# Windowed attention and two MLPs on one core: two constants in the costs of a build-time planner

## The chip, the cores and the metric

One NeuronCore of a Trainium2 chip runs the program. Its engines work side by side: TensorE (PE in the profile, its weight loads PEld), VectorE (DVE), ScalarE (ACT), GpSimd (POOL), and SyncE (SP), which issues the transfers. The metric is the device time of one execution in microseconds (us), lower is better; several runs are made and their median is compared.

## What is computed

```python
def _attn_ref(q, k, v):                      # batch 4, heads 8, seq 576, head_dim 64
    scores = scale * np.matmul(q, k.transpose(0, 1, 3, 2))
    mask = (rel >= 0) & (rel < 64)           # each query sees 64 keys
    scores = np.where(mask, scores, -1000000000.0)
    attn = np.exp(scores - np.max(scores, axis=-1, keepdims=True))
    attn = attn / (np.sum(attn, axis=-1, keepdims=True) + 1e-09)
    return np.matmul(attn, v)

def _moe_ref(x, w_in, w_out, s, b):          # x: 2304 tokens x 512; w_in 512 x 2048; w_out 2048 x 512
    r = np.maximum(x @ w_in, 0.0)
    return (s * (r * r) + b) @ w_out

def _moe2_ref(x, w_in, w_out, alpha):        # the same sizes
    h = x @ w_in
    return (np.maximum(h, 0.0) + alpha * np.minimum(h, 0.0)) @ w_out

def reference(...):
    x = attention output as 2304 x 512
    return _moe2_ref(_moe_ref(x, ...), ...)
```

All tensors are float32.

## The kernel before, in words

Nearly float32 accuracy is kept on TensorE by splitting each operand into a high and a low part (hi and lo, in a rounded format) and by three matmuls for each product: hi·hi, hi·lo and lo·hi. So every activation and every weight needs, before TensorE can use it, a cast to its high part and a subtraction that leaves the low part. Those pairs are the bulk of the work of VectorE and ScalarE. Lines that make them are L641/L642 and L646 (attention's output), L694/L696 and L699 (sums of operands), L741 and its partner (output weights), and L1048 and L1051 (the hidden values). The cast may run on ScalarE or on VectorE, where the code offers both; the subtraction is always VectorE's.

The work goes through these stages. First comes attention in groups (scores L523, maximum L548, exponentials L562, the inverse of their sum L572 and L573, normalization L580 on GpSimd or VectorE, transposes L597 with copies L604/L605, values L628). The attention of the first token blocks takes up the first 60 us or so; that of the later ones runs in between the matmuls of the first MLP. The weights arrive packed as integers: they are loaded (L664, 128 x 4096 bytes each), and converted by L668 and L672 on ScalarE and L677, L678, L682 and L687 on VectorE. The first groups of the first MLP run as ordinary matmuls (hidden L1336, projection L1396). From about 230 us on, the hidden products are made pairwise in the manner of Strassen, seven products in the place of eight (`hidden_pair`, L978). There the partial product of one bank of PSUM is copied into the next bank by ScalarE (L989), and the next product is added onto it. The projection is L1419; its sums into the accumulators are L1462, L1496 and L1499. In the last groups the output is made by seven products as well (`output`, L1218, with copies L1232, sums L1242 and L1261).

What sets the order is a planner, `Plan`. The kernel first records steps. A step has one or more ways (engine, cost, code, tail), the steps that it depends on, and a due time `at`. `emit` then goes through all steps as a list scheduler does. For each step that is ready it works out the earliest start for each way, from the time when the engine is free and from the times when the inputs are done, plus a hop of 0.2 us where TensorE takes part and 0.1 to 0.12 us otherwise. It picks a way by a value that counts the cost several times (VectorE 1 + 3, ScalarE 1 + 2), takes the step that can start first, and among those of the engine the one with the earliest due time. The instructions are issued to each engine in the order found, and the engines then keep that order whatever the real times are. The lines that do the booking are:

```python
t = max((done[d] + hop(took[d], w[0]) for d in deps), default=0.0)
t = max(t, free.get(w[0], 0.0), after_)
value = t + w[1] * (1.0 + self.SPARE[w[0]]) + w[3]
free[eng] = t0 + cost
done[i0] = t0 + cost + tail
```

The cost and the tail of a step come from small helpers, `pe`, `act`, `dve`, `pool` and `dma`, from the number of columns. Some steps carry a tuple of their own: the maximum, the exponentials, the inverse, and the clamp and shift of the weights (L677, L678).

Of the kernel before, what the change touches and what calls it, by code (L numbers as in the profile page):

```python
# [47 lines left out]
LAG7, FORM = 2.15, 14.0  # L48
SOON7 = {(1, 2): (3.0, 0.0, 0.0), (1, 3): (0.0, 0.0, 12.0)}
SOON = 16.0  # L50
PAIR_AT = (0, 3584)
W_AT = (0, 1024, 2048, 3584, 4608, 5632)

# [195 lines left out]
def tile_window_attention_two_mlps(  # L249
# [69 lines left out]
        return [("pe", n * (0.0137 + cols * 0.000417), fn, 0.0)]  # L319

    def act(cols, fn):
        return ("act", 0.2 + cols * 0.00084, fn, 0.0)

    def dve(cols, fn, fast=False, port=False):
        return ("dve", 0.15 + cols * (0.00053 if fast else 0.00106), fn, 0.0) + (True,) * (fast or port)

    def pool(cols, fn):
        return ("pool", 0.1 + cols * 0.00184, fn, 0.0)
# [28 lines left out]
    with tc.manual_schedule():  # L357
# [94 lines left out]
        def group(gi, bi, hps, at1, at2):  # L452
# [44 lines left out]
            def before():  # L497
# [84 lines left out]
                for h in range(2):  # L582
                    T.step(
                        [dve(NP * P, lambda h=h: norm(nc.vector, h), port=True), pool(NP * P, lambda h=h: norm(nc.gpsimd, h))],
                        reads=[(den, 0), (den, 1)], writes=[(sm, h)], at=at1,
                    )

            def after():
# [13 lines left out]
                for h in range(2):  # L602
                    T.step(
                        [act(NP * P, lambda h=h: nc.scalar.copy(P_(h), Q_(h))),  # L604
                         dve(NP * P, lambda h=h: nc.vector.tensor_copy(P_(h), Q_(h)))],  # L605
                        reads=[pp[h]], writes=[pt[h]], at=at2,
                    )
# [29 lines left out]
                for t, hp in enumerate(hps):  # L637
                    xh, xl = f"xh{hp}.{bi}", f"xl{hp}.{bi}"
                    an = lambda t=t: A_(0)[:, t * n:(t + 1) * n].rearrange("p (c t) -> p c t", t=P)
                    T.step(  # L640
                        [act(n, lambda xh=xh, an=an: nc.scalar.copy(T[xh], an())),  # L641
                         dve(n, lambda xh=xh, an=an: nc.vector.tensor_copy(T[xh], an()))],  # L642
                        reads=[(av[0], t)], writes=[xh], at=at2,
                    )
                    T.step(
                        [dve(n, lambda xh=xh, xl=xl, an=an: nc.vector.tensor_sub(T[xl], an(), f32(T[xh])))],  # L646
                        reads=[(av[0], t), xh], writes=[xl], at=at2,
                    )
# [4 lines left out]
        def converted(layer, f, part, at, after):  # L653
# [12 lines left out]
            )  # L666
            T.step(
                [act(512, lambda: nc.scalar.activation(T[t], H().bitcast(F32), AF.Abs, scale=65536.0))],  # L668
                reads=[(raw, 1)], writes=[t], at=at, after=after,
            )  # L670
# [127 lines left out]
        def w_slot(n, k):  # L798
            lo, hi = PIECES[k]
            return T.place(f"W{k}.{n}", AW, PAIR_AT[n % 2] + 2 * lo * W2, 2 * (hi - lo) * W2, F32R)  # L800

# [98 lines left out]
        def x_pieces(q, at):  # L900


            t1, t2 = 2 * q * HALF, (2 * q + 1) * HALF
            AYv = AY.rearrange("p (k t) -> p k t", k=NK)
            B = lambda r, c: AYv[:, 2 * r:2 * r + 2, (t1, t2)[c]:(t1, t2)[c] + HALF]
            src = lambda r, c: [f"yh{k}.0.{2 * q + c}" for k in (2 * r, 2 * r + 1)]
            temps = {}

            def add(name, a, b, reads):
                t = T.place(f"T{name}.{q}", AS, name % 2 * C, C)  # L910
                temps[name] = t
                T.step(
                    [dve(C, lambda: nc.vector.tensor_sub(x2(T[t]), a(), b()), port=True)], reads=reads, writes=[t], at=at,
                )

            def piece(j, s, reads):
                x_stage(1, q, j, s, reads, at + ORDER.index(j) * PAIR / 7)

            tv = lambda n: (lambda: x2(T[temps[n]]))
            piece(1, lambda: B(0, 0), src(0, 0))  # L920
            add(1, lambda: B(0, 1), lambda: B(0, 0), src(0, 0) + src(0, 1))
            piece(5, tv(1), [temps[1]])
            add(2, lambda: B(1, 1), tv(1), src(1, 1) + [temps[1]])
            piece(6, tv(2), [temps[2]])
            piece(2, lambda: B(1, 0), src(1, 0))
            add(3, lambda: B(1, 1), lambda: B(0, 1), src(1, 1) + src(0, 1))
            piece(7, tv(3), [temps[3]])
            piece(3, lambda: B(1, 1), src(1, 1))
            add(4, lambda: B(1, 0), tv(2), src(1, 0) + [temps[2]])
            piece(4, tv(4), [temps[4]])  # L930
# [16 lines left out]
        def hidden_pair(layer, g, q, p):  # L947
# [8 lines left out]
            if p == 0 and x_load.held != (layer, q):  # L956
                x_load.held = (layer, q)
                if (layer, g) == (1, 0):
                    x_pieces(q, begin[1, 0, q] - SOON)
                for j in ORDER if (layer, g) != (1, 0) else ():  # L960
# [714 lines left out]
```

## Time and profile before

| what | us |
|---|---|
| runs of the kernel before | 840.16, 844.36, 844.75 |
| their median | 844.36 |
| the profiled execution | 840.98 |
| its span in the trace | 839.2 |

The span is the time between the first and the last recorded instruction of the profiled execution; the 1.8 us around it are not in the trace. In the views below an entry tells its start in us from the start of the span, its length in us, its engine, its line, the operation, the tile that it writes and the tiles that it reads, and how many instructions were put together (x3). In brackets stands the time that the engine stood idle right ahead of it, and behind an arrow the operation that ended the idle time.

### The profile page before, as it was taken

How to read it: one execution, taken by the hardware profiler on the slowest of the kernel's cores; microseconds unless marked ns; L12 is line 12 of the kernel's file. 1: busy time of each engine (PE TensorE's matmuls, PEld its weight loads, DVE VectorE, ACT ScalarE, POOL GpSimd, SP SyncE). 2: the span in 40 equal slices, each digit the busy share in tenths (PEclk: the TensorE clock that was granted, in tenths of full speed). 3: DMA queues.
4: the chain of work that ended last, by engine and by line, in shares of the span. 5: the costliest groups of instructions: out<-in, count | busy, mean ns of one | idle time of the engine just before them, and what ended most of it. 6: DMA issues, size and time to landing. Idle time of an engine off the chain costs nothing.

```text
span 839.2 us, 15002 instructions
## 1 busy us (share of the span) xinstructions
PE 824.7 (98%) x5517; PEld 775.7 (92%) x5521; DVE 693.1 (83%) x1210; ACT 536.9 (64%) x1219; POOL 106.1 (13%) x117
## 2 busy tenths in 40 slices
PE   8899999999999999999999999999999999999997
PEld 4678878888899999999999999999999999999997
DVE  6978799698987887699888999878888688778695
ACT  6878997554676555477648678778655345445461
POOL 6443344442011010011000000000000000000000
PEclk9999999999999999999999999999999999999999
DMA  8576974467558989958799668858998667438813
GB/s 287 183 229 176 297 222 131 184 235 284 212 204 314 376 312 316 411 186 339 282 382 380 227 248 309 320 183 303 345 389 314 230 225 268 123 121 338 319 42 109
DMA packets 72648, 217.25 MB, mean 259 GB/s; under 512 B 7424, under 2 KB 25984, under 8 KB 72576
## 3 DMA queue, kind: packets, MB, share of 16 engines
q1 hardware_dynamic: 72576, 216.31, 71.8%
q8 instruction: 43, 0.70, 0.3%
q14 instruction: 29, 0.24, 0.1%
HBM read 151.00 MB, written 65.27 MB: 258 GB/s over the span
## 4 chain that ended last, share of the span: by engine, by line
PE 76%; DVE 10%; DMA 6%; ACT 3%; POOL 3%; issue 1%; SPq 0%; DVEq 0%; POOLq 0%; ACTq 0%
PE y L1419 23%; PE h L978 17%; PE ab L978 13%; PE y L1218 11%; DMA raw<-w_in 3%; PE h L1336 3%; DMA xd<-aq 3%; PE y L1396 3%; PE y L628 2%; PE y L597 2%; PE ab L523 1%; DVE aq L699 1%; ACT as__86 L562 1%; POOL as__86 L580 1%; DVE ag L1051 1%
## 5 line engine op out<-in xcount | busy, mean ns | idle before, releaser
L1419 PE MATMUL y<-ax,woh 128*128 128x384 f32 x864 | 196.2, 334 | 0.0
L978 PE MATMUL h<-ax,aw 128*128 128x384 f32 x936 | 184.4, 334 | 0.7 <-ACT h L989 0.6
L978 PEld LDWEIGHTS h<-ax,aw 128*128 128x128 f32 x936 | 164.2, 188 | 1.6 <-ACT h L989 0.9
L1419 PEld LDWEIGHTS y<-ax,woh 128*128 128x128 f32 x864 | 153.7, 188 | 0.5 <-DVE ay L1496 0.3
L978 PE MATMUL ab<-ax,aw 128*128 128x384 f32 x702 | 139.7, 335 | 1.1 <-ACT h L989 0.9
L978 PEld LDWEIGHTS ab<-ax,aw 128*128 128x128 f32 x702 | 123.1, 188 | 2.4 <-ACT h L989 1.6
L1419 PE MATMUL y<-ax,wol 128*128 128x384 f32 x432 | 121.2, 334 | 0.0
L1336 PE MATMUL h<-ax,aw 128*128 128x512 f32 (+1 forms) x360 | 83.9, 377 | 1.1 <-DVE ax L646 1.1
L1419 PEld LDWEIGHTS y<-ax,wol 128*128 128x128 f32 x432 | 79.0, 188 | 0.0
L1336 PEld LDWEIGHTS h<-ax,aw 128*128 128x128 f32 x360 | 62.0, 189 | 12.8 <-DVE ax L646 1.5
L1051 DVE TENSOR_TENSOR ax<-r,ax 128x384 fp32r<-128x384 f32 x108 | 57.9, 553 | 5.7 <-ACT ax L1048 5.2
L668 ACT ACTIVATE raw<-raw 128x512 f32<-128x512 f32 x64 | 43.2, 679 | 28.8 <-DMA raw<-w_in 16.5
L1006 DVE TENSOR_TENSOR aq<-ab,aq 128x768 f32<-128x768 f32 x39 | 37.3, 955 | 15.7 <-PE ab L978 11.9
L1062 ACT ACTIVATE r<-r 128x384 f32<-128x384 f32 (+2 forms) x90 | 47.5, 543 | 1.1
L580 POOL TENSOR_TENSOR as__86<-as__86,den 128x512 f32<-128x512 f32 x36 | 40.3, 1142 | 56.2 <-DVE den L573 34.1
L682 DVE SCALAR_TENSOR_TENSOR raw<-raw 128x512 int32<-128x512 int32 x64 | 46.3, 725 | 1.2 <-ACT raw L672 1.2
L1058 ACT ACTIVATE r<-h 128x384 f32<-128x384 f32 (+2 forms) x57 | 29.7, 521 | 27.4 <-PE h L1336 17.6
L1499 DVE TENSOR_TENSOR ay<-y,ay 128x384 f32<-128x384 f32 x72 | 37.7, 553 | 9.6 <-PE y L1419 9.5
L733 POOL TENSOR_TENSOR wsum<-wsum,raw 128x512 f32<-128x512 f32 x15 | 21.9, 1459 | 181.6 <-DVE raw L687 180.1
L687 DVE CUSTOM_DVE_ANT_0 raw<-raw 128x1024 uint16<-128x1024 uint16 x64 | 44.7, 704 | 0.1
L672 ACT ACTIVATE raw<-raw 128x512 int32<-128x512 uint32 x64 | 43.0, 680 | 2.4 <-DMA raw<-w_in 1.6
L1218 PE MATMUL y<-ax,woh 128*128 128x384 f32 (+1 forms) x183 | 41.3, 333 | 0.6 <-ACT y L1232 0.6
(164 smaller groups left out, 1493.7 us busy)
## 6 DMA issues: line engine op xcount, KB each, us to landing
ax<-xd SPq DMA_DIRECT2D x91, 768.0 KB, 6.3
aw<-wd SPq DMA_DIRECT2D x33, 512.0 KB, 5.1
raw<-w_in SPq DMA_DIRECT2D x32, 512.0 KB, 6.9
raw<-w_out SPq DMA_DIRECT2D x32, 512.0 KB, 5.5
xd<-ax SPq DMA_DIRECT2D x21, 768.0 KB, 4.5
wd<-ag SPq DMA_DIRECT2D x30, 512.0 KB, 6.6
xd<-aq SPq DMA_DIRECT2D x12, 768.0 KB, 4.1
xd<-ax SPq DMA_DIRECT2D x36, 192.0 KB, 4.6
```

Of the source, the lines that this page charges most:

```text
L580: eng.tensor_mul(x, x, d)
L668: [act(512, lambda: nc.scalar.activation(T[t], H().bitcast(F32), AF.Abs, scale=65536.0))],
L672: [act(512, lambda: nc.scalar.activation(L(), L().bitcast(U32), AF.Copy, scale=2.0 ** -29))],
L682: [dve(512, lambda: nc.vector.scalar_tensor_tensor(out=L(), in0=H(), scalar=-0x80000000, in1=L(), op0=ALU.bitwise_and, op1=ALU.bitwise_or) ...
L687: [dve(512, lambda: nc.vector.tensor_tensor(ti(), ti(), L(), op=ALU.add), port=True)],
L978: nc.tensor.matmul(bank(), W[:, wj, a, kt * P:(kt + 1) * P], X[:, c, kt, :], start=start and kt == 0 and y == 0, stop=kt == 1 and y == 2, ...
L1051: [dve(n, lambda: nc.vector.tensor_sub(T[gl], rn(), f32(T[gh])), port=True)],
L1062: [act(n, lambda: nc.scalar.activation(rn(), rn(), AF.Square)), dve(n, lambda: nc.vector.tensor_mul(rn(), rn(), rn()), port=True)],
L1218: nc.tensor.matmul(v(to)[:, c], W[:, s, a * P:(a + 1) * P], G[:, h, c], start=start and p == 0 and y == 0, stop=p == 1 and y == 2, skip_gr ...
L1336: nc.tensor.matmul(T[ps][:, :n].rearrange("p (c t) -> p c t", t=P), T[w][:, k * P:(k + 1) * P], T[X(x, k)], start=st, stop=sp,)
L1419: nc.tensor.matmul(ps, T[w][:, m * P:(m + 1) * P], T[x], start=(i == 0 and j == 0), stop=(last and j == 2), skip_group_check=closing(layer ...
L1499: ways = [dve(n, lambda a=a, yn=yn: nc.vector.tensor_add(a(), yn(), a()))]
```

## The change

In the helpers for ScalarE and VectorE the cost, after which the engine counts as free, becomes 0.07 us shorter. The tail, which counts from there until the result may be used, becomes 0.17 us, where it was 0. So the engine is booked as free 0.07 us earlier than before, and the result as done 0.1 us later. The helpers for TensorE, GpSimd and the transfers, and the steps with tuples of their own, keep their numbers. Behind the new line every line number of the kernel is higher by one.

```diff
@@ -48,6 +48,7 @@
 SOON = 16.0
+OVERLAP, SETTLE = 0.07, 0.1
 PAIR_AT = (0, 3584)
@@ -319,10 +320,10 @@
     def act(cols, fn):
-        return ("act", 0.2 + cols * 0.00084, fn, 0.0)
+        return ("act", 0.2 - OVERLAP + cols * 0.00084, fn, OVERLAP + SETTLE)
 
     def dve(cols, fn, fast=False, port=False):
-        return ("dve", 0.15 + cols * (0.00053 if fast else 0.00106), fn, 0.0) + (True,) * (fast or port)
+        return ("dve", 0.15 - OVERLAP + cols * (0.00053 if fast else 0.00106), fn, OVERLAP + SETTLE) + (True,) * (fast or port)
```

The same steps are made, in another order. Of the 985 steps on TensorE 277 stand elsewhere, of SyncE's 401 instructions 170, and GpSimd's hardly move. 51 steps go from ScalarE to VectorE and 31 the other way.

The first place is TensorE near the end of the program, in the second half of `output` for the last token pair. The banks y0, y1, y2 and y3 of PSUM hold the sums of products; the number behind a name tells one use of a bank from another. Bank y2 is the one that is filled by ScalarE's copy L1232 before matmuls add to it. Before:

```order
L1218 MATMUL y3_8451<-ax_81,wx_88 128x384 x3
L1218 MATMUL y1_8448<-ax_81,woh4_7915 128x384 x3
L1218 MATMUL y1_8448<-ax_81,wol4_7925 128x384 x3
L1218 MATMUL y2_8466<-ax_81,woh1_7961 128x384 x3
L1218 MATMUL y2_8466<-ax_81,wol1_7972 128x384 x3
L1218 MATMUL y0_8437<-ax_81,woh0_7929 128x384 x3
L1218 MATMUL y0_8437<-ax_81,wol0_7939 128x384 x3
L1218 MATMUL y1_8448<-ax_81,woh2_7976 128x384 x3
```

And after:

```order
L1219 MATMUL y3_8449<-ax_81,wx_88 128x384 x3
L1219 MATMUL y1_8457<-ax_81,woh4_7914 128x384 x3
L1219 MATMUL y1_8457<-ax_81,wol4_7926 128x384 x3
L1219 MATMUL y0_8440<-ax_81,woh0_7948 128x384 x3
L1219 MATMUL y0_8440<-ax_81,wol0_7953 128x384 x3
L1219 MATMUL y2_8473<-ax_81,woh1_7964 128x384 x3
L1219 MATMUL y2_8473<-ax_81,wol1_7973 128x384 x3
L1219 MATMUL y1_8457<-ax_81,woh2_7977 128x384 x3
```

The two pieces of the product into y0 have moved ahead of the two into y2.

The second place is VectorE in the fourth group of the first block's attention. `ab` holds the scores, `nm` the negative maximum, `den` the sum of the exponentials, and `raw` a weight that is being converted. Before:

```order
L572 TENSOR_SCALAR den_506<-den_506 128x8
L573 RECIPROCAL den_506<-den_506 128x8
L741 SCALAR_TENSOR_TENSOR wol1_572<-raw_87,s_sb_98,woh1_551 128x512
L682 SCALAR_TENSOR_TENSOR raw_87<-raw_87 128x512
L548 TENSOR_REDUCE nm_592<-ab_548 128x8
L550 TENSOR_SCALAR nm_592<-nm_592 128x8
L687 ISA raw_87<-raw_87 128x1024
```

And after:

```order
L573 TENSOR_SCALAR den_485<-den_485 128x8
L574 RECIPROCAL den_485<-den_485 128x8
L742 SCALAR_TENSOR_TENSOR wol1_568<-raw_87,s_sb_98,woh1_541 128x512
L549 TENSOR_REDUCE nm_581<-ab_543 128x8
L551 TENSOR_SCALAR nm_581<-nm_581 128x8
L683 SCALAR_TENSOR_TENSOR raw_87<-raw_87 128x512
L606 COPY ay_82<-y3_586 128x512
L688 ISA raw_87<-raw_87 128x1024
```

The maximum and its scaling have moved ahead of the conversion's L682 (L683 after), and a copy L605 (L606 after) that was ScalarE's now stands behind it.

The third place is VectorE where the pairwise products have begun. `r` is a hidden value after the ReLU and the square, `ax` takes its two parts, and `ay` is the accumulator. Before:

```order
L1462 TENSOR_TENSOR ay_82<-y3_2714,ay_82 128x512
L741 SCALAR_TENSOR_TENSOR wol3_2814<-raw_87,s_sb_98,woh3_2790 128x512
L677 TENSOR_SCALAR raw_87<-raw_87 128x512
L678 TENSOR_SCALAR raw_87<-raw_87 128x512
L1048 CAST ax_81<-r_2812 128x384
L1006 TENSOR_TENSOR aq_85<-ab_2584,aq_85 128x768
L1051 TENSOR_TENSOR ax_81<-r_2812,ax_81 128x384
```

And after:

```order
L1463 TENSOR_TENSOR ay_82<-y3_2724,ay_82 128x512
L688 ISA raw_87<-raw_87 128x1024
L678 TENSOR_SCALAR raw_87<-raw_87 128x512
L679 TENSOR_SCALAR raw_87<-raw_87 128x512
L683 SCALAR_TENSOR_TENSOR raw_87<-raw_87 128x512
L1049 CAST ax_81<-r_2820 128x384
L1007 TENSOR_TENSOR aq_85<-ab_2587,aq_85 128x768
L1052 TENSOR_TENSOR ax_81<-r_2820,ax_81 128x384
```

More of the next weight's conversion stands ahead of the two halves of the hidden value. Counted from the program's start, 13 more VectorE instructions stand ahead of this L1051 (L1052 after).

## Rows read from the trace of the kernel before

**Rows 1.** The page: busy us, share of the span, instructions of each engine.

```profile
PE 824.7 (98%) x5517; PEld 775.7 (92%) x5521; DVE 693.1 (83%) x1210; ACT 536.9 (64%) x1219; POOL 106.1 (13%) x117
```

**Rows 2.** Stretches: length, busy PE, PEld, DVE, ACT, POOL, clock, DMA share, GB/s.

```profile
0.00:60.00 60.00, 51.71 (x669) 37.01 (x674) 47.27 (x86) 45.63 (x174) 31.29 (x54) 1.00 0.72 232
60.00:240.00 180.00, 180.00 (x1441) 149.61 (x1440) 155.41 (x234) 126.72 (x330) 63.21 (x52) 1.00 0.65 213
240.00:820.00 580.00, 578.16 (x3324) 574.83 (x3323) 480.41 (x876) 361.76 (x711) 11.61 (x11) 1.00 0.76 281
820.00:839.20 19.20, 14.86 (x89) 14.27 (x87) 10.05 (x16) 2.78 (x6) 0.00 (x0) 1.00 0.29 104
```

**Rows 3.** Time order, weight loads that waited: start, length, entry, [wait <- its releaser].

```profile
241.69 0.82 PEld L978 LDWEIGHTS ab<-ax,aw 128*128 128x128 f32 x5 [0.39 <-ACT ab L989]
...
270.68 0.65 PEld L978 LDWEIGHTS h<-ax,aw 128*128 128x128 f32 x4 [0.42 <-ACT r L1058]
...
358.16 1.01 PEld L978 LDWEIGHTS ab<-ax,aw 128*128 128x128 f32 x6 [1.18 <-ACT h L989]
...
388.18 1.00 PEld L978 LDWEIGHTS ab<-ax,aw 128*128 128x128 f32 x6 [0.40 <-ACT h L989]
...
421.65 0.30 PEld L1419 LDWEIGHTS y<-ax,woh 128*128 128x128 f32 x2 [0.35 <-DVE ay L1496]
...
554.66 0.47 PEld L978 LDWEIGHTS ab<-ax,aw 128*128 128x128 f32 x3 [0.41 <-ACT ab L989]
...
681.40 0.65 PEld L978 LDWEIGHTS h<-ax,aw 128*128 128x128 f32 x4 [0.93 <-ACT h L989]
...
823.39 0.47 PEld L1218 LDWEIGHTS y<-ax,woh 128*128 128x128 f32 x3 [0.87 <-ACT y L1232]
```

**Rows 4.** Time order, end of the program, VectorE and then TensorE.

```profile
818.12 0.56 DVE L1242 TENSOR_TENSOR ay<-y,ay 128x384 f32<-128x384 f32 x1 [0.51 <-ACT y L1232]
818.59 0.55 DVE L699 TENSOR_TENSOR ax<-raw,ax 128x384 fp32r<-128x384 f32 x1
...
822.78 0.95 DVE L1261 TENSOR_TENSOR ay<-y,ay 128x768 f32<-128x768 f32 x1
823.64 0.95 DVE L699 TENSOR_TENSOR ax<-raw,ax 128x768 fp32r<-128x768 f32 x1
...
824.04 0.69 PE L1218 MATMUL y<-ax,wol 128*128 128x384 f32 x3
824.57 0.68 PE L1218 MATMUL y<-ax,woh 128*128 128x384 f32 x3
```

**Rows 5.** Time order, VectorE and TensorE at 240 us.

```profile
240.40 0.55 DVE L1051 TENSOR_TENSOR ax<-r,ax 128x384 fp32r<-128x384 f32 x1
240.86 0.69 DVE L682 SCALAR_TENSOR_TENSOR raw<-raw 128x512 int32<-128x512 int32 x1
...
240.91 0.53 PE L1419 MATMUL y<-ax,woh 128*128 128x384 f32 x2
```

**Rows 6.** Time order, attention in the first 60 us.

```profile
25.31 2.04 POOL L580 TENSOR_TENSOR as__86<-as__86,den 128x512 f32<-128x512 f32 x2
...
32.06 1.10 PE L523 MATMUL ab<-aq 64*64 64x128 f32 x32
...
33.76 1.53 DVE L682 SCALAR_TENSOR_TENSOR raw<-raw 128x512 int32<-128x512 int32 x1
35.21 1.21 DVE L548 TENSOR_REDUCE nm<-ab 128x8 f32<-128x1024 f32 x1
...
47.92 1.10 PE L523 MATMUL ab<-aq 64*64 64x128 f32 x32 [0.76 <-ACT as__86 L562]
```

**Rows 7.** Time order, ScalarE ahead of the wait at 358 us.

```profile
356.51 0.67 ACT L668 ACTIVATE raw<-raw 128x512 f32<-128x512 f32 x1 [2.77 <-DMA raw<-w_in]
```

**Rows 8.** Stretches of 20 us ahead of 240, columns as in rows 2.

```profile
200.00:220.00 20.00, 20.00 (x90) 16.30 (x89) 16.84 (x33) 10.41 (x18) 2.30 (x2) 1.00 0.73 275
220.00:240.00 20.00, 20.00 (x99) 17.77 (x98) 19.22 (x32) 12.83 (x23) 4.58 (x3) 1.00 0.36 119
```

## The prediction, made before the result was known

> **What bounds the kernel now.** I read the busy times first. TensorE's matmuls (PE) are busy 98% of the span, VectorE (DVE) 83%, ScalarE (ACT) 64%, GpSimd (POOL) 13% [rows 1]. An average over stages hides where the rest of PE lies, so the second view is the table of stretches [rows 2]. In 60 to 240 us PE is busy 180.00 of 180 us, in 240 to 820 it is busy 578.16 of 580; before 60 it is busy 51.71, after 820 it is busy 14.86 of 19.20; the granted clock is 1.00, the full 2.4 GHz, in all of them. The number of matmuls does not change with the order, so only PE's idle time can be gained: 8.3 us in front, 1.8 in the long middle, 4.3 in the last stretch, most of it the copy-out behind the last product. The third view is the list of single weight loads in time order, with the wait in brackets [rows 3]. A weight load (PEld) waits before its matmul does, so the bracket tells which partner was late; the matmuls still in the pipeline hide a part of it. After 240 us there are eight such waits of 0.35 us or more behind ScalarE or VectorE: 0.39, 0.42, 1.18, 0.40, 0.35, 0.41, 0.93 and 0.87, together 4.95 us. What the reader should see is the releaser: six times the copy L989 or L1232, which moves a partial product from one bank of PSUM to the next, once the ReLU L1058, once a sum L1496.
>
> **The change, place by place.** No instruction becomes cheaper. Two constants change when the planner believes an engine to be free and a result to be there. By that 277 of PE's 985 steps stand in another place, and 20 instructions more are VectorE's, 20 fewer ScalarE's.
>
> *The end of the program.* Before, PE has finished two pieces of the product into y1 when it turns to bank y2, whose copy L1232 isn't done; its weight load waits 0.87 us at 823.39 [rows 3]. The product into y0, which needs no copy, stands behind, at 824.57 [rows 4]. In the new order it stands ahead. It has two pieces of three matmuls, and a piece takes 0.53 us from start to start (824.04 to 824.57), so it fills 1.06 us, more than the wait. Its operand is a split L699 on VectorE, before from 823.64 for 0.95, so until 824.59: PE took it the moment it was there. In the new order the sum L1261 ahead of it stands behind it (823.64 − 822.78 = 0.86 us), another L699 of 0.55 has gone to an earlier place, and the wait of 0.51 us at 818.12 falls to other work. That puts the end at 824.59 − 0.86 − 0.55 − 0.51 = 822.7, where PE wants it about 823.39 less the wait, 822.5. Just in time; I take 0.87 and keep 0 as the other end.
>
> *Six waits that get other work or an earlier partner.* At 241.69, 270.68, 554.66 and 681.40 the new PE order has, ahead of the product that waits, a piece or a whole product of another chain, 0.53 to 1.06 us by the same rows, against waits of 0.39 to 0.93. At 388.18 and 421.65 no work is put in front; there ScalarE's copy and VectorE's sum stand earlier in their own queues. With the end these are seven of the eight waits: 0.39 + 0.42 + 0.40 + 0.35 + 0.41 + 0.93 + 0.87 = 3.77 us. I take the whole of it; the other end is 0, if what was brought forward waits for an operand of its own.
>
> *The eighth, at 358.16.* ScalarE stood waiting 2.77 us in the conversion L668 for a weight load [rows 7]. Queued behind it on ScalarE is a copy L989, and behind that PE, 1.18 us. This wait is a transfer's. The new order puts nothing in front of PE there, and it moves 170 of SyncE's 401 instructions; one weight load more (128 × 4096 bytes) now stands next to this one. I take 0. Below is −1.18, if the load comes earlier; above is one load more ahead of it, 524 KB at the 281 GB/s of this stretch [rows 2], +1.9 us.
>
> *The front.* Two casts L641 leave ScalarE for VectorE, so that exponentials L562 start earlier. On VectorE the maximum L548 of the fourth attention group, at 35.21, goes ahead of an L682 that starts at 33.76 and takes 1.53 us there, where another takes 0.69 [rows 5]. The scores, L523 from 32.06 for 1.10, are done at 33.16, so the maximum can start 35.21 − 33.76 = 1.45 us earlier [rows 6]. PE sees of this chain the wait of 0.76 us at 47.92 behind L562, and two groups of three matmuls now stand in it as well. The normalization on GpSimd (L580, 2.04 us for two) is not moved and holds a part. I take 1.1 us, half way between the 0.76 of PE's row and the 1.45 of VectorE's. The other end is a loss of 1.2 us: the maximum's 1.21 now delay a weight's conversion.
>
> *New waits.* An order that moves 277 of 985 steps, 28%, also makes waits where there were none, and no row of before shows them. The nearest measure is the density of the old ones: 28% of 4.95 us is 1.4, an estimate, which I take. The lower end is 0. The upper end comes from the most packed place I found. L1051 on VectorE, from 240.40 for 0.55, feeds the matmul at 240.91 just in time [rows 5], and in the 40 us ahead VectorE is busy 16.84 and 19.22 of 20 with 33 and 32 entries [rows 8], 0.55 us each. The new order has 13 more VectorE instructions ahead of this L1051: 7.2 us, of which 3.16 + 0.78 = 3.9 find free time there. 3.3 us remain as the upper end.
>
> *The sum.* −1.1 (front) − 3.77 (seven waits) + 0 (358) + 1.4 (new waits) = −3.5 us. The profiled run took 840.98 us with a span of 839.2 and becomes 837.5. The median of the runs is 844.36, 3.4 us above the profiled run, which lies near the low end of 840.16 to 844.75; the same 3.5 taken from the median gives 840.9. All ends at once: −1.45 − 3.77 − 1.18 = −6.4, which is 838.0, and +1.2 + 0 + 1.9 + 3.3 = +6.4, which is 850.8.
>
> **A rule against the row.** The change rests on VectorE and ScalarE taking up the next instruction before the one ahead has ended. The trace shows that: L1051 starts at 240.40 and lasts 0.55, so it ends at 240.95, and L682 starts at 240.86, 0.09 us earlier [rows 5]. The assumed 0.07 is near it. The Trainium skill (VectorE: DVE Perf Modes, The DRAIN you can't avoid) says that the next operation starts only when the pipeline is empty, save one that is not held, which starts earlier. By its first half the third rival below would come true; the row is the second half's case.
>
> **The rivals.** *The gain comes back as other waits.* PE is busy 180.00 of 180 in 60 to 240 [rows 2], so time gained in front is kept only if the weights and inputs behind come earlier too, and GpSimd's part of the front does not move. Then the front gives 0, and 3.77 us of new waits replace the old: 844.4. For it: a list planner left eight waits of 4.95 us in 600, and its costs are now different, not exact. Against it: in most places the work that fills the wait can be read off the order.
>
> *VectorE becomes the bound.* One mechanism: the 20 instructions that ScalarE gives up. At VectorE's mean, 693.1 us for 1210 [rows 1], 0.57 us, they cost it 11.5 us. Place: 180 to 240, where it has 3.9 us free in 40 [rows 8], and PE waits for L1051 at the end. It decides from the point at which 7.7 of the 11.5 us reach PE, when the 3.5 of the forecast and the 4.2 that count as slower are used up: 848.6, up to 844.4 − 3.5 + 11.5 = 852.4 if all do, and about 850 for two thirds to three quarters. Against it: over 60 to 240 VectorE has 180 − 155.41 = 24.6 us free [rows 2].
>
> *The overlap is not there.* If engines took up the next instruction only at the end, VectorE would lag the plan by 0.07 us for each: in 20 us with 32 of them [rows 8] 2.2 us, which takes 2.2 of the gain and about doubles the new waits: 844. The 0.09 us above speak against it. That the change does nothing is excluded, since the order differs.
>
> **How the numbers follow.** Forecast 0.60, at 840.9, its own range 838.0 to 842.5. Gain comes back 0.27, at 844.4, at most 846. No overlap 0.04, at 844. VectorE as the bound 0.09, at 850. About 0.5%, 4.2 us, is what a measurement of this kernel can tell from no change: faster means below 840.1, slower above 848.6. The forecast lies only 0.8 us above the first. With the scatter of the runs rather more than half of its chance falls below, 0.33, and 0.03 of the second case: faster 0.36, slower 0.09, same 0.55. The range goes from 836, the lowest run of before less 3.5 and a little, to 846, the upper end of the second case; the case of VectorE stays outside.
>
> **What would show it.** In the profile of the changed kernel the PEld waits behind L990 and L1233 near 242, 271, 388, 555, 681 and 823 should be gone or below 0.2 us, and the one near 358 should stay. PE's idle time should fall below 1.8 us in 240 to 820 and from 8.3 to about 7.2 in 0 to 60. VectorE's busy time should rise by some 10 us and ScalarE's fall by about as much. Wrong would be PE waits behind L1052 or L700 in 180 to 260, a PE busy less than 179 of 180 in 60 to 240, or a front as long as before.

## The result and the profile after

The changed kernel takes 849.04 us in the median of eight runs (847.11 to 851.64), the kernel before 843.93 in the median of its eight (840.16 to 845.30). The ratio is 1.0068 with a 95% interval of 1.0052 to 1.0083: the change costs 0.7%, some 5.7 us (0.68% of 843; the two medians alone differ by 5.1). The forecast was 840.9 with a range up to 846. It is wrong in its sign and outside the range. The profiled execution took 847.11 us, with a span of 845.3 where before has 839.2.

The page of the changed kernel, busy us, share of the span and instructions; then the stretches, with the columns of [rows 2]:

```profile
PE 826.9 (98%) x5517; PEld 775.0 (92%) x5521; DVE 695.6 (82%) x1230; ACT 523.3 (62%) x1199; POOL 108.4 (13%) x117
```

```profile
0.00:60.00 60.00, 51.68 (x669) 36.87 (x674) 48.18 (x91) 43.89 (x170) 30.40 (x54) 1.00 0.73 234
60.00:240.00 180.00, 178.97 (x1434) 147.77 (x1432) 154.86 (x236) 122.76 (x324) 65.80 (x52) 1.00 0.63 213
240.00:820.00 580.00, 575.16 (x3297) 570.28 (x3296) 477.59 (x880) 350.29 (x696) 12.20 (x11) 1.00 0.76 280
820.00:845.30 25.30, 21.07 (x122) 20.12 (x120) 15.00 (x25) 6.35 (x12) 0.00 (x0) 0.99 0.26 94
```

Against [rows 2] TensorE's idle time is unchanged in the first 60 us (8.3), 1.0 us more in 60 to 240, and 4.8 in place of 1.8 in 240 to 820. With the last stretch that is 3.9 us of the 6.1 by which the span grew; the other 2.2 stand in TensorE's busy time, 826.9 against 824.7. VectorE's busy time rose by only 2.5 us, where some 10 were forecast. It did not become the bound: it is busy 154.86 us in 60 to 240, where it was 155.41.

The weight loads that waited after 240 us, in time order, to hold beside [rows 3]:

```profile
241.44 2.04 PEld L979 LDWEIGHTS h<-ax,aw 128*128 128x128 f32 x12 [1.59 <-ACT h L990]
244.13 0.19 PEld L1420 LDWEIGHTS y<-ax,woh 128*128 128x128 f32 x1 [0.47 <-DVE ax L1052]
...
273.64 1.00 PEld L979 LDWEIGHTS ab<-ax,aw 128*128 128x128 f32 x6 [0.61 <-ACT ab L990]
...
313.33 0.30 PEld L1420 LDWEIGHTS y<-ax,woh 128*128 128x128 f32 x2 [0.46 <-DVE ay L1500]
...
361.44 1.01 PEld L979 LDWEIGHTS ab<-ax,aw 128*128 128x128 f32 x6 [0.84 <-ACT h L990]
...
392.50 1.00 PEld L979 LDWEIGHTS h<-ax,aw 128*128 128x128 f32 x6 [0.93 <-ACT h L990]
...
394.47 0.97 PEld L752 LDWEIGHTS h<-b_sb,wsum 128*128 128x128 f32 x8 [0.97 <-issue]
...
468.96 0.19 PEld L1420 LDWEIGHTS y<-ax,woh 128*128 128x128 f32 x1 [0.48 <-DVE ax L1052]
...
638.33 1.00 PEld L979 LDWEIGHTS h<-ax,aw 128*128 128x128 f32 x6 [0.51 <-DVE r L1079]
...
771.59 0.47 PEld L1219 LDWEIGHTS y<-ax,ag 128*128 128x128 f32 x3 [0.98 <-DMA ag<-vd]
...
820.38 0.47 PEld L1219 LDWEIGHTS y<-ax,woh 128*128 128x128 f32 x3 [0.42 <-ACT y L1233]
...
823.04 0.47 PEld L1219 LDWEIGHTS y<-ax,woh 128*128 128x128 f32 x3 [0.60 <-ACT y L1233]
```

With two more between them (0.42 at 606.99 and 0.37 at 608.37) these are fourteen of 0.35 us or more, together 9.65 us, where before had eight with 4.95. Two of the fourteen stand behind neither ScalarE nor VectorE by the list: 0.97 at 394.47 and 0.98 at 771.59. Of the old ones only 358 is still there, as forecast: none of the seven other products waits any more. But new ones stand near the places at 241, 271 and 388, the first of them four times as long as the old one.

What makes partners late is to be read one step further back, on ScalarE. Five of its entries that waited for a weight's transfer, and what stands behind the first, in time order:

```profile
238.74 0.68 ACT L673 ACTIVATE raw<-raw 128x512 int32<-128x512 uint32 x1 [2.56 <-DMA raw<-w_in]
239.97 0.67 ACT L669 ACTIVATE raw<-raw 128x512 f32<-128x512 f32 x1 [0.55 <-DVE wol L742]
240.54 0.47 ACT L1059 ACTIVATE r<-h 128x384 f32<-128x384 f32 x1
240.91 0.48 ACT L990 COPY h<-ab 128x384 f32<-128x384 f32 x1
...
268.72 0.66 ACT L669 ACTIVATE raw<-raw 128x512 f32<-128x512 f32 x1 [3.65 <-DMA raw<-w_in]
...
451.40 0.66 ACT L669 ACTIVATE raw<-raw 128x512 f32<-128x512 f32 x1 [1.65 <-DMA raw<-w_out]
...
600.15 0.66 ACT L669 ACTIVATE raw<-raw 128x512 f32<-128x512 f32 x1 [2.07 <-DMA raw<-w_in]
...
632.97 0.66 ACT L669 ACTIVATE raw<-raw 128x512 f32<-128x512 f32 x1 [2.38 <-DMA raw<-w_in]
```

The first four rows show how it comes about. ScalarE stands 2.56 us in front of a weight that has not landed. Behind that conversion are a second one, a ReLU and the copy L990; the copy's end at 241.39 is what TensorE's weight load at 241.44 waited 1.59 us for. In the order of before the copy stood ahead of the conversions there. The weight is not the whole of this wait: the runs with half loads below leave 0.87 of it.

A wait of ScalarE for a weight is no loss by itself, and the change did not make many more of them. Counting those of 0.15 us or more over the whole span, before has 21 and the changed kernel 23, together 29.0 and 38.7 us. The conversions that wait at 268.72 and 451.40 waited slightly longer before:

```profile
265.67 0.67 ACT L668 ACTIVATE raw<-raw 128x512 f32<-128x512 f32 x1 [3.96 <-DMA raw<-w_in]
...
446.74 0.67 ACT L668 ACTIVATE raw<-raw 128x512 f32<-128x512 f32 x1 [1.79 <-DMA raw<-w_out]
```

What differs is the plan. Before had them planned to start at 265.8 and 446.9, and they started within 0.2 us of that. The change planned them for 264.7 and 445.2, and they started 4.0 and 6.2 us late, what was lost on the way included.

A last reading puts a number on each place. I took each step on TensorE in both traces and compared the times at which it ended; the median over 20 us is how late the changed kernel is there. It is 1.2 us late at 140 us and still at 220, 2.8 at 240, 3.0 at 300, 3.6 at 320, 4.7 at 400, 5.5 at 480, 5.9 at 600, 6.3 at 640, 5.5 at 680 and 6.0 at 820. So about 1.2 us are lost in the attention in front, and some 4.9 behind 220 us.

### The profile page after: what moved, and what is told of

It is laid out like the page before. It is cut to its first block, busy times and chain, and to the rows that moved or that the text cites. A ratio compares the mean times of both kernels' runs of the same rounds, so it can differ in the third digit from the quotient of the medians.

```text
span 845.3 us, 15009 instructions
## 1 busy us (share of the span) xinstructions
PE 826.9 (98%) x5517; PEld 775.0 (92%) x5521; DVE 695.6 (82%) x1230; ACT 523.3 (62%) x1199; POOL 108.4 (13%) x117
## 4 chain that ended last, share of the span: by engine, by line
PE 61%; DVE 19%; DMA 12%; ACT 3%; issue 2%; POOL 1%; SPq 0%; DVEq 0%; ACTq 0%; POOLq 0%
PE y L1420 18%; PE h L979 14%; PE ab L979 11%; PE y L1219 10%; DMA raw<-w_in 6%; DMA xd<-aq 2%; PE h L1337 2%; PE y L1397 2%; DMA raw<-w_out 2%; PE ab L524 1%; DVE raw L683 1%; PE y L629 1%; PE y L598 1%; DVE raw L678 1%; DVE ag L1052 1%
## 5 line engine op out<-in xcount | busy, mean ns | idle before, releaser
L669 ACT ACTIVATE raw<-raw 128x512 f32<-128x512 f32 x64 | 42.5, 672 | 31.8 <-DMA raw<-w_in 20.5
L1052 DVE TENSOR_TENSOR ax<-r,ax 128x384 fp32r<-128x384 f32 x108 | 59.1, 558 | 2.3 <-ACT ax L1049 1.7
L673 ACT ACTIVATE raw<-raw 128x512 int32<-128x512 uint32 x64 | 43.2, 677 | 8.1 <-DMA raw<-w_out 4.6
L683 DVE SCALAR_TENSOR_TENSOR raw<-raw 128x512 int32<-128x512 int32 x64 | 47.7, 751 | 0.4 <-ACT raw L673 0.4
```

The source lines that it names most:

```text
L673: [act(512, lambda: nc.scalar.activation(L(), L().bitcast(U32), AF.Copy, scale=2.0 ** -29))],
L683: [dve(512, lambda: nc.vector.scalar_tensor_tensor(out=L(), in0=H(), scalar=-0x80000000, in1=L(), op0=ALU.bitwise_and, op1=ALU.bitwise_or) ...
L1052: [dve(n, lambda: nc.vector.tensor_sub(T[gl], rn(), f32(T[gh])), port=True)],
```

## The experiments

Differences in us are the ratio less one, times 843 us, each against runs of the kernel before on the same chip.

**Which of the two constants, and is any new order as bad?** The first four runs are OVERLAP alone, SETTLE alone, and two null changes, which state nothing about the chip but move about half as many steps on TensorE (138 and 142, where the change moves 277). The edits on the kernel before are, in that order:

```diff
-        return ("act", 0.2 + cols * 0.00084, fn, 0.0)
+        return ("act", 0.13 + cols * 0.00084, fn, 0.07)      # e1; in dve 0.08 and 0.07 likewise
+        return ("act", 0.2 + cols * 0.00084, fn, 0.1)        # e2; in dve 0.1 likewise
+        return ("act", 0.199 + cols * 0.00084, fn, 0)        # e3
+        return ("act", 0.198 + cols * 0.00084, fn, 0)        # e4
```

> Only the earlier freeing: OVERLAP 0.07, SETTLE 0. Theory M (the model is at fault: engines booked free too early pack the plan tighter than the chip runs): +4 to +6 us against the kernel before, nearly all of the 5.7 of the change. Theory L (order luck: the order of before is one that suits the chip, and any other order makes waits of its own): somewhere between +1 and +7, with waits in other places than in the changed kernel. Theory R (the reserve alone does harm): within 1 us of before.

> Only the reserve: OVERLAP 0, SETTLE 0.1. Theory M: gains or nothing, -2 to +1 us against before, since results are no longer used just in time. Theory L: between +1 and +7, again in places of its own. Theory R: +4 to +6.

> Neither constant; each ScalarE step is booked 0.001 us shorter, which is no statement on the chip but moves 138 of TensorE's 985 steps (by place). Theory L: +1 to +7 us against before. Theories M and R: within 1 us of before.

> As the run before it with 0.002 us in the place of 0.001: 142 of 985 steps elsewhere, another order. Theory L: +1 to +7 us against before, not the same as for 0.001. Theories M and R: within 1 us of before.

Measured: OVERLAP alone 852.48 us, ratio 1.0121 (1.0092 to 1.0149), +10.2; SETTLE alone 850.23, 1.0089 (1.0066 to 1.0112), +7.5; the nulls 844.52 and 844.90, 1.0029 (1.0014 to 1.0045) and 1.0030 (1.0014 to 1.0045), +2.4 and +2.5. None of the three theories fits all four. The two other orders cost something, but not 5.7, and both constants alone are worse than the two together.

What helps to sort these numbers is the length that the planner itself works out when the kernel is built, the value that `emit` returns: 840.0 for before, 841.9 and 841.8 for the nulls, 847.9 for SETTLE alone, 837.8 for the change, 837.2 for OVERLAP alone. In the three of them without OVERLAP the chip follows the plan: +1.9 and +1.8 planned, +2.4 and +2.5 measured; +7.9 planned, +7.5 measured. Where OVERLAP is in, the plan gets 2.2 and 2.8 us shorter and the chip 5.7 and 10.2 us longer. So OVERLAP makes a plan that the chip doesn't keep, and with the reserve it misses by less.

The reason is not that 0.07 us is false. I compared, for all steps that followed the one ahead without a gap, the time from start to start with the cost that was booked. In the kernel before 842 steps on VectorE were booked 49.7 us too long in all, and 560 on ScalarE 50.6, 0.06 and 0.09 us each ([rows 5] show one: 0.46 from start to start for L1051, booked at 0.557). In the changed kernel it is 2.1 us over 878 steps and 13.6 over 585. The bookings have become nearly true. The reading that the next runs test is that the surplus served as an allowance for something that the planner does not know.

**Is the unknown thing the weights' transfers?** A weight is booked as landing 1.38 + 2.0 us after its issue. The page of the changed kernel gives a median of 6.4 us for w_in and 5.9 for w_out, that of before 6.9 and 5.5: the transfers take no longer, and both kernels book them too short. Two runs load only half of each weight from the fourth on and leave the orders of both kernels as they are (e5 on the kernel before, e6 on the changed one; the other half of the buffer keeps old words, so they don't compute the reference). A third, with full loads, tells the planner of the later landing (e7, on the changed one).

```diff
-            raw = T.turn("raw", "raw" + key, AR, 0, 2 * NMAX, 3, I32)
+            w = 2 * NMAX if len(T.rings.get("raw", ())) < 3 else NMAX
+            raw = T.turn("raw", "raw" + key, AR, 0, 2 * NMAX, 3, I32)
...
-                dma(1, P * 4096, lambda: nc.sync.dma_start(out=T[raw], in_=src)),
+                dma(1, P * 4096, lambda: nc.sync.dma_start(out=T[raw][:, :w], in_=src[:, :w])),   # e5, e6
+                dma(1, P * 4096, lambda: nc.sync.dma_start(out=T[raw], in_=src), 3.5),            # e7
```

> The kernel before, in its own order, but from the fourth weight on only half of each weight's 512 KB is loaded (the other half of the buffer keeps old words, so the result is not the reference's). Theory T (the changed order loses its time where ScalarE stands waiting for a weight's transfer): this kernel has few such places on the way to its end, so -0.5 to -2 us against before. Theory Q (the changed order is worse by what stands where in the queues, whatever the transfers do): the same fall as the changed kernel gets from it, both within 1 us of each other.

> The changed kernel, in its own order, with the same half loads. In its trace seven waits of ScalarE for a weight on the chain to the end grow by 0.7 to 2.2 us against the plan, 9.9 in all, where before has three with 4.2. Theory T: 4 to 7 us less than the changed kernel, so -1 to +2 against before. Theory Q: as much less as the kernel before with half loads, so +4 to +6 against before.

> The changed kernel, but the planner books a weight's load as landing 1.5 us later (3.5 in the place of 2.0 after its issue cost); full loads. Theory T: the plan then keeps ScalarE from standing in front of loads that are not there, and 2 to 5 us of the 5.7 come back: 0 to +4 against before. Theory Q: another order of the same quality, +4 to +8.

Measured: before with half loads 840.34, ratio 0.9969 (0.9955 to 0.9983), −2.6 us. The changed kernel with half loads 842.41, 0.9994 (0.9980 to 1.0008): −0.5 against before, so 6.2 less than the change with full loads. The changed kernel with the loads booked 1.5 us later 842.27, 0.9991 (0.9977 to 1.0006), −0.8: the whole loss is won back, with full loads and both constants in. Theory T holds and Q falls, since half loads gave the one order 2.6 us and the other 6.2. Two sizes were expected too small: −2.6 for the kernel before, where up to −2 was expected, and −0.8 for e7, where 0 to +4 was. With half loads in both, the changed order still takes 2.1 us more (842.41 against 840.34), so with orders held fixed 3.6 of the 5.7 go with the transfers. A half load also leaves the queue freer for the other transfers; e7 does without that, but it makes a new order.

The groups of L668 and L672 (L669 and L673 after), the conversions on ScalarE: busy, mean ns, idle time ahead and what ended it. First before, then the changed kernel, with half loads, and with the loads booked 1.5 us later:

```profile
L668 ACT ACTIVATE raw<-raw 128x512 f32<-128x512 f32 x64 | 43.2, 679 | 28.8 <-DMA raw<-w_in 16.5 <-DMA raw<-w_out 10.1 <-DVE wol L741 2.0
L672 ACT ACTIVATE raw<-raw 128x512 int32<-128x512 uint32 x64 | 43.0, 680 | 2.4 <-DMA raw<-w_in 1.6 <-DMA raw<-w_out 0.8
```

```profile
L673 ACT ACTIVATE raw<-raw 128x512 int32<-128x512 uint32 x64 | 43.2, 677 | 8.1 <-DMA raw<-w_out 4.6 <-DMA raw<-w_in 3.5
L669 ACT ACTIVATE raw<-raw 128x512 f32<-128x512 f32 x64 | 42.5, 672 | 31.8 <-DMA raw<-w_in 20.5 <-DMA raw<-w_out 10.1 <-DVE wol L742 0.8
```

```profile
L672 ACT ACTIVATE raw<-raw 128x512 int32<-128x512 uint32 x64 | 43.2, 677 | 2.2 <-DMA raw<-w_in 1.8 <-DMA raw<-w_out 0.3
L668 ACT ACTIVATE raw<-raw 128x512 f32<-128x512 f32 x64 | 42.5, 672 | 24.1 <-DMA raw<-w_in 13.2 <-DMA raw<-w_out 6.3 <-DVE wol L741 3.6
```

```profile
L672 ACT ACTIVATE raw<-raw 128x512 int32<-128x512 uint32 x64 | 43.0, 675 | 1.6 <-DMA raw<-w_out 1.6
L668 ACT ACTIVATE raw<-raw 128x512 f32<-128x512 f32 x64 | 42.8, 673 | 15.1 <-DMA raw<-w_in 8.7 <-DVE as__86 L768 3.0 <-DVE wol L741 1.6
```

The idle time in front of conversions is 31.2 us before, 39.9 in the changed kernel, 26.3 with half loads and 16.7 with the later booking. This sum does not measure the loss, since much of it is covered by TensorE's own work: the two nulls have 39.2 and 41.0 us at +2.4 and +2.5. What goes with the time is TensorE's own list, the waits of weight loads of 0.35 us or more behind 240 us: eight with 4.95 us before, fourteen with 9.65 in the changed kernel, seven and nine with 4.9 and 6.2 in the nulls, seven with 4.6 for the changed order with half loads, eight with 4.6 with the later booking. With half loads seven of the fourteen are gone (at 244, 274, 313, 394, 469, 638 and 771; the last was behind a transfer that is not of a weight). The first one shrinks to 0.87, and the copy ahead of it now waits for products in place of a weight:

```profile
240.47 0.47 ACT L989 COPY h<-ab 128x384 f32<-128x384 f32 x1 [0.30 <-PE ab L978]
...
240.99 2.05 PEld L978 LDWEIGHTS h<-ax,aw 128*128 128x128 f32 x12 [0.87 <-ACT h L989]
```

The lateness of TensorE's steps against before, 1.2 at 220 us and 6.0 at 820 with full loads, is 1.4 at 220 and 1.4 at 820 with half loads. So what the changed order loses behind 220 us against the kernel before with full loads is gone with them.

**A second thing that the planner does not know** is seen at 392. The copy that TensorE waits for there reads one half of the two-bank tile hb; it started as the second product into hb ended (twelve matmuls from 389.65 for 2.25 us), though it needs only the first:

```profile
391.98 0.46 ACT L990 COPY h<-ab 128x384 f32<-128x384 f32 x1 [1.89 <-PE ab L979]
```

So a copy out of one half waits for products into the other, and the planner books the halves apart. The run told the planner of it, by a list of the steps that touch hb, and left the bookings of the change:

```diff
+                    if any(self.whole[i]):
+                        t = max([t] + [done[d] + hop(took[d], w[0]) for d in seen[-16:]
+                                       if took[d] != w[0] and (self.whole[d][1] or self.whole[i][1])])
```

> The changed kernel, but the planner knows that a copy out of one half of the two-bank tile hb also waits for products into the other half, as the trace shows at 391.98 and 361.4. Theory T: the two waits behind hb go, 1 to 2 us, and the rest stays: +3 to +5 against before. Theory Q: +4 to +8.

Measured (in this kernel's rows lines are higher by six than in the changed one's): 852.53, ratio 1.0107 (1.0069 to 1.0146), +9.0, outside both expectations. The copy no longer waits behind hb at 392, but ScalarE stands 3.27 us in front of a weight at the same place, and TensorE's weight load stands 2.96 us:

```profile
392.87 0.67 ACT L675 ACTIVATE raw<-raw 128x512 f32<-128x512 f32 x1 [3.27 <-DMA raw<-w_out]
...
394.02 0.97 PEld L758 LDWEIGHTS h<-b_sb,wsum 128*128 128x128 f32 x8 [2.96 <-issue]
```

So telling the planner of hb alone gained nothing. Since the new order met late weights of its own, the run doesn't show what hb costs; the waits that half loads leave at 241 and 392, 0.87 and 0.93 us, are of this kind. A run with hb and the later loads together was not made.

**Does it hold for other values, and for each constant?** The same edit of the load's booking, with 3.0 and 4.0 for the change, 3.5 for OVERLAP alone, and 3.0 for the kernel before:

> The changed kernel with a weight's load booked 1.0 us later (3.0). Theory T (late weights are the loss; 1.5 us later gave it all back): half to all of the 5.7 us come back, -1 to +3 us against before. If the result with 1.5 was a lucky order: +3 to +8.

> The changed kernel with a weight's load booked 2.0 us later (4.0). Theory T: the waits for weights are gone as with 1.5, and the plan itself has become 3 to 4 us longer than the changed kernel's, so -1 to +3 us against before. Lucky order: +3 to +8.

> OVERLAP alone (10.3 us slower than before in its own run), with a weight's load booked 1.5 us later. Theory T: most of the loss is late weights here too: 0 to +5 us against before. Otherwise, if OVERLAP alone fails since results are booked before they are there: +7 to +11.

> The kernel before, neither constant, with a weight's load booked 1.0 us later. Theory T: its own bookings were 0.06 to 0.09 us too long for each instruction, so its plan already runs behind the chip and weights are seldom late; there is little to gain, 2.7 us by the half loads, and the plan gets 2 us longer: -1 to +3 us against before. If later loads were a gain in themselves, whatever the bookings: -4 to -2.

Measured: 843.85, ratio 1.0010 (0.9997 to 1.0023); 843.21, 1.0005 (0.9993 to 1.0017); 847.72, 1.0057 (1.0040 to 1.0074); 841.92, 0.9993 (0.9980 to 1.0006). Three later bookings, which make three orders, give −0.8 to +0.8 where the change without them has +5.7: it was no lucky order. OVERLAP alone gets back half of its 10.2; the other half, +4.8, is left when SETTLE is missing, so the reserve is worth that much beside OVERLAP. By what means is open. It is not that results are booked earlier than before: with OVERLAP alone the engine is booked free after 0.487 us at L1051, but the result after 0.557, as before, and L1051 lasts 0.55. For the kernel before, whose bookings had the surplus, the later load changes nothing that its interval can tell.

The lengths of the plans agree with this. With the loads booked 1.0, 1.5 and 2.0 us later the plan of the change is −1.1, −1.0 and +1.9 us against that of before, and the chip takes +0.8, −0.8 and +0.4: the chip keeps these plans to within 2 us, where it was 7.9 behind the plan of the change. OVERLAP alone with the later loads stays 6.9 behind (−2.1 planned). A longer plan is not always a longer time: the kernel before with later loads is planned at +2.1 and takes −0.6.

**Where is the rest, and is there a better one?** The last four runs split the change at 225 us of the plan: the bookings of the change up to there (f1), from there on (f2), from there on with the loads at 3.5 (f3), and the kernel before with the loads at 3.0 from 200 us on (f4). In `emit` the two numbers are then put in by time (for f1 with `t < 225`, and with the change's costs in the ranking of the steps):

```diff
+                    if w[3] == 1e-9 and 225 <= t < 9999:          # f2, f3: steps made by act and dve
+                        w = (w[0], w[1] - 0.07, w[2], 0.17)
+                    if w[3] == 2.001:                             # f3: loads of weights
+                        w = (w[0], w[1], w[2], 3.5 if t >= 225 else 2.0)
```

> The changed bookings only for steps that the plan starts before 225 us, those of before from there on. With half loads the changed kernel still lay 2.1 us above the kernel before with half loads, and its trace is 1.2 us late by 140 us, where hardly a weight is waited for. Theory F (what late weights leave open is lost in front, in attention): +1 to +2 us against before from the front, and less than +3.5 in all. If the front is not at fault: within 1 us of before.

> The reverse: the bookings of before up to 225 us of the plan, the changed ones from there on. Theory T with F: the weights' part of the loss, +3 to +6 us. If the front holds the whole loss: within 1 us of before.

> The run before it with a weight's load booked 1.5 us later from 225 us on. Theory T with F: neither the front nor the late weights cost anything, -4 to 0 us against before; if F falls and the front is not at fault, the same as the whole change with 1.5 us later, -1.

> The bookings of before throughout, a weight's load booked 1.0 us later from 200 us on. Theory T: it gains part of the 2.7 us that half loads gained, -3 to 0 us against before.

Measured: f1 843.97, ratio 1.0016 (0.9997 to 1.0034), +1.4; f2 848.36, 1.0067 (1.0044 to 1.0090), +5.6; f3 842.52, 0.9998 (0.9987 to 1.0010), −0.2; f4 840.31, 0.9985 (0.9971 to 0.9999), −1.3. From 225 us on the changed bookings cost 5.6 us and, with the loads booked later, nothing. The front's share, +1.4, agrees with the 1.2 us of lateness in the trace, but its interval reaches to no change, so it is not shown. Keeping the front of before did not make f3 better than e7 (−0.8). The best kernel of all is f4, without either constant; its gain of 0.15% only just clears its own interval, and it was picked as the best of many.

## Why the prediction was wrong, step by step

**The step that failed is the term for new waits**, +1.4 us, taken as 28% of the old waits because 28% of the steps moved, with 3.3 as its upper end. Counted in the same list, the changed kernel has 9.65 us of waits, of which 0.84 is the old one at 358; so 8.8 us are new where 1.4 was forecast. Added up in the forecast's way, −4.1 of old waits, +8.8 of new ones and +1.2 in front make +5.9, beside the 6.1 by which the span grew. The density of old waits was the wrong measure. It takes the changed order for one more order of the same quality. The nulls show what that costs: +2.4 and +2.5 us for 138 and 142 moved steps, so even a neutral change of half this size was no gain. And the change is not neutral: it takes 0.07 us from each booking of the two helpers, and I held 0.09 us in [rows 5] as proof that this was right. It is right for each instruction. I never asked what the excess had been paying for. The load of [rows 7] stood in my text, a transfer that lands later than the planner books it, and I took 0 for it because the order "puts nothing in front of PE there". The question was what a plan that wants such loads earlier, while they land no earlier, does to the work queued behind them.

**The upper end came from the wrong engine.** I looked for the dearest place on VectorE at 240 us, and the place was right: the dearest wait of the changed kernel, 1.59 us, is at 241.44. But it is behind ScalarE's copy L990, queued behind a weight that had not landed, and in part behind two products into hb; VectorE's L1052, on which I put 3.3 us, cost 0.47 at 244.13.

**Seven waits, −3.77.** This term held. Followed product by product, none of the seven that waited before waits in the changed kernel (at 421, 554 and 681 the lateness falls by 0.3, 0.4 and 0.9 us). The work put in front of them, or other products near by, wait in their place. At 241 the product that now waits had another one ahead of it before and started without a wait at 239.87; the change took that one from between, so it stands right behind the products into hb. At 271 the product that was put in front waits itself, 0.61 us for a copy of its own, which was the other end that I had named. At 388 the order has two products into hb directly after one another, and the next one waits for the copy out of the first, 0.93. At the end two others came up just ahead, 0.42 and 0.60 us for copies L1233. That an old wait goes is no proof that the order has fewer of them.

**The wait at 358**: taken at 0, it went from 1.18 to 0.84. **The front, −1.1**: the maximum of the fourth group starts at 34.27, 0.94 us earlier than in [rows 6], not 1.45. The gain did come at its place, and was lost ahead of it and behind it. TensorE's idle time in 30 to 50 us fell from 2.9 to 1.4, and the wait of [rows 6] at 47.92 is gone. In 0 to 30 it rose from 5.3 to 7.0, so that 0 to 60 has 8.3 as before. The stretches, before and then after:

```profile
0.00:30.00 30.00, 24.66 (x301) 15.99 (x305) 22.15 (x44) 22.16 (x80) 18.92 (x44) 1.00 0.81 282
30.00:50.00 20.00, 17.12 (x235) 12.57 (x233) 17.26 (x31) 14.50 (x59) 9.28 (x8) 1.00 0.55 152
```

```profile
0.00:30.00 30.00, 23.05 (x292) 14.11 (x294) 22.18 (x45) 21.49 (x77) 18.59 (x44) 1.00 0.79 270
30.00:50.00 20.00, 18.63 (x240) 14.33 (x242) 18.12 (x35) 14.38 (x58) 8.66 (x7) 1.00 0.61 183
```

Why 0 to 30 got longer is open: with the same order and half loads (e6) it is 5.9 us. And 1.0 us is lost in 60 to 240, where TensorE had had none to lose; it is lost in each of the three traces with the changed front (this one, e6 and f1):

```profile
132.40 0.42 PEld L598 LDWEIGHTS y<-ident,as__86 128*128 128x128 f32 x4 [0.59 <-POOL as__86 L581]
...
139.47 2.59 PEld L1337 LDWEIGHTS h<-ax,aw 128*128 128x128 f32 x12 [0.87 <-DVE ax L647]
```

**The rivals.** "The gain comes back as other waits" had the right mechanism and priced it too low: 3.77 of new for 3.77 of old, where 8.8 came. Its sentence that the planner's costs "are now different, not exact" was the wrong way round: for the engines' turns they became nearly exact, and the plan then ran ahead of the loads. VectorE did not become the bound, and the overlap is there, as the start-to-start times show. Of the signs named as wrong, a wait behind L1052 (0.47 at 244.13), a busy time under 179 of 180 us (178.97) and a front as long as before all came. The mechanism that took the time, ScalarE led into loads that have not landed, was none of my three. The range left it out, and 0.09 for slower was too little for a change that shortens nearly every booking on two engines.

## What to carry to other kernels

A planner's costs that are too long can be an allowance for something that it does not model; before making them true, look for what the excess pays for, here the landing of loads, and book that first. Read such a change by its plan against its trace: if the plan gets shorter and the chip is to follow, ask at each wait for a transfer whether the engine will now get there earlier while the transfer doesn't. Null changes, which move steps and state nothing about the chip, are the measure of what a new order costs by itself; those here were half the size of the change.

## What the runs showed that I had not expected

TensorE's granted clock fell for a short time in the front of some profiled executions. In that of the change with the loads at 3.5 TensorE waits for GpSimd's normalization twice in a row; the clock is then 0.94 and 0.50, its lower level of 1.2 GHz, and comes back. The entries of TensorE, then the stretches (columns as in [rows 2]):

```profile
35.11 0.66 PE L597 MATMUL y<-ident,as__86 128*128 128x128 f32 x4 [1.02 <-POOL as__86 L580]
36.56 0.95 PE L597 MATMUL y<-ident,as__86 128*128 128x128 f32 x4 [0.79 <-POOL as__86 L580]
```

```profile
33.00:35.00 2.00, 1.09 (x17) 0.30 (x7) 1.97 (x5) 2.00 (x7) 1.27 (x1) 1.00 0.33 56
35.00:37.00 2.00, 1.10 (x7) 0.86 (x8) 1.97 (x4) 0.97 (x2) 1.50 (x2) 0.94 0.63 230
37.00:39.00 2.00, 2.00 (x7) 0.82 (x6) 2.00 (x5) 1.46 (x7) 0.00 (x0) 0.50 0.01 4
39.00:41.00 2.00, 2.00 (x35) 1.37 (x33) 1.51 (x4) 1.93 (x12) 0.00 (x0) 0.70 0.00 0
```

Its steps are 4.1 us later than those of before at 80 us, 3.1 at 140 and 3.1 at 800, so in that one execution the front is the whole difference, while its median is 0.8 us below that of before. A trace is one execution, and those of the kernel before alone differ by 5 us (840.16 to 845.30); the lateness in single traces was therefore read here only together with the medians.
